# Value loads of a decode attention kernel issued from ScalarE's queue instead of SyncE's

## The chip, the core and the metric

The kernel runs on one core of a Trainium2 chip. The core has a matrix engine (TensorE, PE in the profile), VectorE (DVE), ScalarE (ACT), GpSimd (POOL) and SyncE (SP), each with its own instruction stream, and 16 DMA engines that move data from the device's memory (HBM) to the on-chip memory SBUF. SyncE and ScalarE can both issue DMAs; the profile calls SyncE's DMA queue q1 and ScalarE's q10. An engine's instructions run in order, so an engine that waits for a semaphore holds up everything behind the wait. The metric is the device time of one execution in microseconds (us). Three runs of the kernel before gave 1324.48, 1324.66 and 1324.93 us.

## The reference

Two attention branches, A and B, work on the same one-token input and are mixed by a gate:

```python
def branch(x, k_cache, v_cache, wq, wo):             # x (2, 1, 512), caches (2, 32, 4096, 128)
    q = (x @ wq).reshape(B, 1, 32, 128).transpose(0, 2, 1, 3)
    scores = einsum("bhqd,bhkd->bhqk", q, k_cache) * 128 ** -0.5
    o = einsum("bhqk,bhkd->bhqd", softmax(scores), v_cache)
    return o.transpose(0, 2, 1, 3).reshape(B, 1, 4096) @ wo

g = sigmoid((x * gate_w).sum(-1, keepdims=True))
out = g * branch(x, A_...) + (1 - g) * branch(x, B_...)
```

There is one query per head, and no key or value is used twice: 2 branches x 2 batch rows x 32 heads x 4096 tokens x 128 floats, for keys and for values, are read once each. With the four weight matrices of 8.39 MB that makes 570.43 MB.

## The kernel before

**Units.** The work is cut into 32 units, numbered 0 to 31: branch A first, then B; within a branch eight groups of four heads, and for each group the two batch rows. So an even unit is batch row 0 of a group, the odd unit after it batch row 1 of the same group. A unit has one load of keys, K(u), and one of values, V(u). Each is 4 heads x 4096 tokens x 128 floats, 8.39 MB, laid out as 128 partitions with one contiguous row of 64 KB in each.

**Tiles.** Keys have two tiles, `kt0` and `kt1`, used in turn by even and odd units. Values have one, `vt`. The same three tiles hold weights at the ends: `wq` of A and B lies in the key tiles before the first keys, `wo` of A and B in `kt0` and `kt1` after the last keys.

**What a unit does.** VectorE multiplies the key tile by the spread-out query in place (L391) and adds along the head dimension (L394); as soon as that is done it raises `k_free` for the tile. It then finds the maximum (L399 to L401) and raises `maxima`. ScalarE, on `maxima`, computes the four exponentials (L365) into `padded` and raises `weights`. TensorE, in the loop `products`, waits for `weights` and for `v_landed`, multiplies `padded` and the value tile in 32 chunks into the PSUM tile `vp` (L369; the profile shows two matmuls for each chunk), and raises `summed`. ScalarE, on `summed`, clears the used part of `padded` (L431), and tells that `vt` is free.

**Pairs.** After an odd unit ScalarE also takes the first quarter of the result out of `vp` (L452, `take_out`) and raises `taken`. VectorE, after scoring the *next* even unit, waits for `taken`, adds the other three quarters (L415, `add_out`), raises `added`, and only then looks for the maximum of the even unit and starts the next scoring. ScalarE clears `vp` on `added` (L459). So VectorE can be at most one unit ahead of the products at that point. In the middle of an even unit, between its two long instructions, VectorE waits for `spare`, which ScalarE raises after the products of the even unit before.

**The order of loads.** All large loads are issued by SyncE, in one list written out by hand: `wq` A, `wq` B, K0, K1, V0, then K2, V1, K3, V2 and so on to K31, V30, then `wo` A, V31 in three pieces (1/2, 3/8 and 1/8 of it), `wo` B in six pieces. Ahead of each K(u) SyncE waits for the `k_free` of unit u - 2, ahead of each V(u) for `v_free`, which says that V(u - 1) was used up. While SyncE waits for one tile, the loads behind it in the list aren't issued. ScalarE issues two small loads at the start (`A_x` and `gate_w`) and half of the output at the end.

**The end.** When the last products are done, VectorE, TensorE and ScalarE gather the heads, deal them out into rows and multiply by `wo` of B, whose pieces arrive last; the results are copied out and stored.

Of the kernel before, what the change touches and what calls it, by code (L numbers as in the profile page):

```python
# [12 lines left out]
P = 128  # L13
B = 2
# [4 lines left out]
G = 4  # L19
PH = P // G  # L20
NG = H // G
NS = SK // PH
NH = NS // 4
# [22 lines left out]
class Streams:  # L46
# [32 lines left out]
    def put(self, e, make, reads=(), writes=(), gives=None):  # L79

        self.before(e, reads, writes)
        i = make(self.engines[e])
        if gives is not None:
            i.then_inc(gives, 1)
            return None
        self.ticks[e] += 1
        i.then_inc(self.sems[e], 1)
        point = self.sems[e], self.ticks[e]
        self.after(point, reads, writes)
        return point  # L90
# [51 lines left out]
def tile_gated_decode(ctx: ExitStack, tc: tile.TileContext, ins: dict, out: bass.AP):  # L142
    nc = tc.nc
# [5 lines left out]
    NU = len(units)  # L149
# [5 lines left out]
    slot = small.tile([P, VC], F32, name="slot")  # L155
# [14 lines left out]
    vt = big.tile([P, NS, DH], F32, name="vt")  # L170
# [8 lines left out]
    with tc.tile_critical():  # L179
        S = Streams(nc, tc)  # L180
# [3 lines left out]
        r_vt = R()  # L184
# [6 lines left out]

        sem = tc.alloc_semaphore
        v_landed, k_landed = sem("v_landed"), [sem(f"k_landed{i}") for i in range(2)]
        v_free, k_free = sem("v_free"), [sem(f"k_free{i}") for i in range(2)]
        weights, summed = sem("weights"), sem("summed")
        maxima, taken, added, spare = sem("maxima"), sem("taken"), sem("added"), sem("spare")
        D_, A_ = Round(S, "dve"), Round(S, "act")


        def tokens(cache, u):  # L200
            n, g, b = units[u]
            rows = ins[n + cache].rearrange("b h s d -> (b h s) d")
            r0 = (b * H + g * G) * SK
            return rows[r0:r0 + G * SK].rearrange("(p r) d -> p r d", p=P)
# [2 lines left out]
            [("wq", "A"), ("wq", "B"), *(("k", u) for u in range(NU)), ("wo", "A"), ("wo", "B")])}  # L207
        parts = {}

        def load_parts(item, t, src, slots, *cuts):  # L210
            parts[item] = [S.dma("sp", t[:, i:j], src[:, i:j], slot=s) for s, i, j in zip(slots, cuts, cuts[1:])]

        def arrived(e, item, *which):
            p = parts[item]
            S.wait(e, [p[k] for k in which] if which else p)
# [6 lines left out]
        def load_k(u):  # L222
            if u == 0:
                S.before("sp", [], r_kt[0])
                load_parts(("k", 0), kt[0], tokens("_k_cache", 0), "de", 0, NS // 2, NS)
                return
            if u == 1:
                S.before("sp", [], r_kt[1])
            else:
                nc.sync.wait_ge(k_free[u % 2], u // 2)  # L230
            nc.sync.dma_start(kt[u % 2], tokens("_k_cache", u)).then_inc(k_landed[u % 2], 16)

        def load_v(u):
            if u == 0:
                S.before("sp", [], [r_vt])
            else:
                nc.sync.wait_ge(v_free, u)
            if u < NU - 1:
                nc.sync.dma_start(vt, tokens("_v_cache", u)).then_inc(v_landed, 16)
            else:  # L240
                load_parts(("v", u), vt, tokens("_v_cache", u), "deg", 0, NS // 2, NS - NH // 2, NS)

        def load_wo(n):
            i = place["wo", n]
            nc.sync.wait_ge(k_free[i], NU // 2)
            t = kt[i].rearrange("p r d -> p (r d)").rearrange("p (r e) -> p r e", e=D)
            for r in r_kt[i]:
                r.writers, r.readers = [], []
            load_parts(("wo", n), t, ins[n + "_wo"].rearrange("(p r) e -> p r e", p=P), *(
                ("f", 0, OR) if n == "A" else ("abchij", 0, OR // 2, 3 * OR // 4, EARLY, OR - 2, OR - 1, OR)))  # L250


        class Scratch:
# [3 lines left out]
            def take(self, n):  # L257
                self.at += -(-n // 128) * 128
                return self.t[:, self.at - -(-n // 128) * 128:][:, :n]

        start = Scratch(vt).take
        rows, ident, ones, xg, w, e = start(D), start(P), start(1), start(B * KC), start(P), start(1)
# [3 lines left out]
        def vput(e, make, reads=(), writes=(), **kw):  # L266
# [6 lines left out]
                                  slot="y"))  # L273
# [87 lines left out]
        def exps(u, b, col, do):  # L361

            s, m = sc[u % 2], nm[u % 2]
            for j, h in enumerate(QUARTERS):
                do(lambda x: x.activation(padded[h, :, b, j * VC:(j + 1) * VC], s[h].rearrange("p (c a) -> p c a", a=VC),  # L365
                                          AF.Exp, bias=m[h], accum_out=lp[h, col]), weights if j == G - 1 else None)
# [40 lines left out]
        def dve_second(nxt):  # L407
            take("dve", k_landed[1], 16)
            maxima_of(1, whole_scores(1, 0))
            return next_queries(*nxt, 0) if nxt else 0  # L410
# [19 lines left out]
        def clear_padded(b):  # L430
            return A_.do(lambda x: x.activation(padded[:, :, b], nil[:, :, None].to_broadcast([P, NVC, G * VC]), AF.Copy))  # L431

        def act_exps(u, b, col):
            take("act", maxima)
            exps(u, b, col, lambda make, gives: A_.do(make, 0, gives))

        def act_second(col, last=False):
            take("act", summed)
            at = clear_padded(0)
            A_.tell(v_free, at)  # L440
            A_.tell(spare, at)
            if not last:
                act_exps(1, 1, col)
                return
            A_.close()
            take("act", maxima)
            exps(1, 1, col, lambda make, gives: put("act", make, [], [R()]))
            r_lp.writers = r_pad.writers = [(S.sems["act"], S.ticks["act"])]

        def take_out(g):  # L450
            take("act", summed)
            A_.do(lambda x: x.activation(vs[:, g], vp[:, :DH], AF.Copy, scale=slot[:, :1]), 0, taken)  # L452

        def act_first(g, col, between=None):
            take_out(g)
            at = clear_padded(1)
            A_.tell(v_free, at)
            take("act", added)
            A_.do(lambda x: x.activation(vp, nil.to_broadcast([P, VC * DH]), AF.Copy))  # L459
            if between:  # L460
                between()
            act_exps(0, 0, col)
            A_.close()
# [12 lines left out]
        def deal_out(n):  # L476
            t = vs[:, 0]
            put("act", lambda x: x.activation(t, heads, AF.Copy, scale=rs), [r_heads, r_rs], [r_vs[0]])
            dealt = bank[:, :B * OR].rearrange("p (b r) -> p b r", b=B)
            for b in range(B):  # L480
                for k in range(DQ):
                    put("pe", lambda x: x.matmul(dealt[:, b], deal[:, b, k].rearrange("p g h q -> p (g h q)"),
                                                 t[:, k * OR:(k + 1) * OR], start=k == 0, stop=k == DQ - 1),
                        [r_deal, r_vs[0]], [r_bank])
            put("act", lambda x: x.activation(on[n], dealt.rearrange("p b r -> p r b"), AF.Copy), [r_bank], [r_on[n]])
# [31 lines left out]
        load_k(0)  # L517
        project("B")
        load_k(1)
        load_v(0)  # L520
        for u in range(2, NU):
            load_k(u)
            load_v(u - 1)
        load_wo("A")
        load_v(NU - 1)
        load_wo("B")

        spread_queries(0)
        for h in (0, 1):
            t = kt[0][:, h * NS // 2:(h + 1) * NS // 2]  # L530
            r = R()
# [16 lines left out]
        def dve_pairs(n):  # L548
            S.wait("dve", [*r_q.writers, (S.sems["dve"], S.ticks["dve"])])
            with nc.Fori(0, NG - 1, engines=[mybir.EngineType.DVE]) as i:  # L550
                nxt = n, bass.ds(i + 1, 1)
                at = dve_second(nxt)
                dve_first(i, nxt, at)

        def act_pairs():
            with nc.Fori(0, NG - 1, engines=[mybir.EngineType.Activation]) as i:
                act_second(bass.ds(i * B + 1, 1))
                act_first(i, bass.ds(i * B + B, 1))

        products(NU // 2)  # L560
        dve_pairs("A")
        act_pairs()
        at = dve_second(("B", slice(0, 1)))
        act_second(slice(PH // 2 - 1, PH // 2))

        def branch_sums():
            sum_of("A")
# [2 lines left out]
                gather(g)  # L570

        dve_first(NG - 1, ("B", slice(0, 1)), at, branch_sums)
        act_first(NG - 1, slice(0, 1), lambda: deal_out("A"))
        products(NU // 2 - 1)
        project_out("A", OR)
        dve_pairs("B")
        act_pairs()
        dve_second(None)
        act_second(slice(PH // 2 - 1, PH // 2), last=True)
        D_.close()  # L580

        end = Scratch(kt[place["wo", "A"]]).take
# [33 lines left out]
        for i, e in enumerate(("dve", "act")):  # L616
            for j in range(STRIPS // OS):
                k = (i * STRIPS // OS + j) * QT
                src = acc[i][k:k + B, :D // STRIPS]
# [27 lines left out]
```

## Time and profile before

| | |
|---|---|
| median of 3 runs | 1324.66 us (1324.48 to 1324.93) |
| profiled execution, its own time | 1324.58 us |
| its span, first to last instruction | 1322.8 us |
| VectorE busy | 1166.3 us (88%) |
| TensorE busy with matmuls | 343.3 us (26%) |
| ScalarE busy | 101.4 us (8%) |
| read from HBM | 570.43 MB, 431 GB/s over the span |
| q1 (SyncE's loads) | 99.6% of the time of the 16 DMA engines |
| mean granted TensorE clock | 0.627 |

Times in timelines are microseconds from the start of the span, first the start and then the duration. In rows of instructions the names stand as output<-input; an x and a number is a count; the bracket at the end gives the idle time of the engine ahead of the instruction and what ended it. SPq and ACTq are the moments at which SyncE and ScalarE issue a DMA, not the transfer. In the list of DMA issues the last number is the median time from issue to landing. DVEq, ACTq and PEq as releasers stand for an engine's own instruction stream, in which a wait for a semaphore sits. L95 and L132 are helpers that wait and signal, so rows that name them tell which engine was waited for, not for which step.

### The profile page before, as it was taken

The page shows a single profiled execution, that of the slowest core. Times are in us where ns is not written, and L with a number is a line of the kernel's source. Part 1 is how long each engine was busy: PE and PEld are TensorE (multiplying, and loading weights), DVE is VectorE, ACT ScalarE, POOL GpSimd, SP SyncE. Part 2 cuts the span into 40 slices and gives each one's busy share as a digit, 9 for nine tenths or more (in the row PEclk, how much of TensorE's full clock was granted, in tenths as well). Part 3 has the DMA queues.
Part 4 walks back from the last instruction along what each step waited for, and adds up shares of the span by engine and source line. Part 5 has one row for each costly group of instructions (what it writes and reads, how often), then busy time and mean ns, then how long its engine had stood idle before and what let it go on. Part 6 is the DMA issues. An engine that isn't in the chain of part 4 may idle for free. (4 is left out here: it accounts for less than half of the span.)

```text
span 1322.8 us, 6257 instructions
## 1 busy us (share of the span) xinstructions
PE 343.3 (26%) x2406; PEld 100.7 (8%) x2406; DVE 1166.3 (88%) x321; ACT 101.4 (8%) x331; POOL 1.2 (0%) x8
## 2 busy tenths in 40 slices
PE   3202222202222221222224022222212222221256
PEld 0000000000000000000002000000000000000012
DVE  2399999999999999999999899999999999999960
ACT  0000000001010000101000010100001010000100
POOL 0000000000000000000000000000000000000000
PEclk9656666556666655666665566666566666656668
DMA  9999999999999999999999999999999999999998
GB/s 412 442 414 442 442 416 442 444 414 444 442 430 428 442 442 416 442 442 416 444 442 419 438 442 434 426 440 440 420 440 440 420 442 442 426 432 442 434 420 357
DMA packets 11109, 570.53 MB, mean 431 GB/s; under 512 B 1239, under 2 KB 1243, under 8 KB 1630
## 3 DMA queue, kind: packets, MB, share of 16 engines
q1 hardware_dynamic: 11092, 570.43, 99.6%
q8 instruction: 4, 0.07, 0.0%
q14 instruction: 3, 0.02, 0.0%
q10 hardware_dynamic: 10, 0.01, 0.0%
HBM read 570.43 MB, written 0.00 MB: 431 GB/s over the span
## 5 line engine op out<-in xcount | busy, mean ns | idle before, releaser
L391 DVE TENSOR_TENSOR kt<-kt,q 128x16384 f32<-128x16384 f32 x31 | 534.0, 17226 | 56.1 <-DVEq L95 56.0
L394 DVE TENSOR_REDUCE sc<-kt 128x128 f32<-128x16384 f32 x31 | 533.8, 17220 | 1.1
L369 PE MATMUL vp<-vt,pr 128*32 128x512 f32 x2048 | 291.8, 733 | 919.3 <-PEq L95 918.5
L369 PEld LDWEIGHTS vp<-vt,pr 128*32 128x32 f32 x2048 | 80.3, 132 | 1129.3 <-issue 1126.9
L365 ACT ACTIVATE pr<-sc,nm 32x128 f32<-32x128 f32 x128 | 50.9, 398 | 160.0 <-ACTq L95 118.2
L431 ACT ACTIVATE pr<-nil 128x512 f32<-128x512 f32 x31 | 19.3, 624 | 426.4 <-ACTq L95 426.4
L452 ACT ACTIVATE vs<-vp,slot 128x128 f32 (+1 forms) x16 | 5.9, 368 | 451.6 <-ACTq L95 451.6
L339 PE MATMUL qa<-kt,cols 128*2 128x512 f32 x128 | 18.7, 741 | 22.9 <-DMA kt<-in_B_wq_dram 15.7
L365 ACT ACTIVATION_READ_ACCUMULATOR pr<-sc,nm (+1 forms) x128 | 23.5, 184 | 0.0
L350 DVE STREAM_TRANSPOSE kt<-kt 128x1024 f32<-128x1024 f32 x1 | 1.2, 1246 | 23.5 <-ACT kt L348 23.5
L415 DVE SCALAR_TENSOR_TENSOR vs<-vp,slot,vs 128x128 f32 (+1 forms) x45 | 15.8, 351 | 6.3 <-DVEq L95 5.3
L534 DVE TENSOR_REDUCE sc<-kt 128x64 f32<-128x8192 f32 x2 | 17.4, 8686 | 0.1
L533 DVE TENSOR_TENSOR kt<-kt,q 128x8192 f32<-128x8192 f32 x2 | 17.4, 8686 | 0.0
L459 ACT ACTIVATE vp<-nil 128x512 f32<-128x512 f32 x15 | 9.0, 600 | 106.6 <-ACTq L95 106.6
L621 DVE COPY kt<-qa 2x128 f32<-2x128 f32 x2 | 0.6, 280 | 17.0 <-PE qa L512 17.0
L592 DVE TENSOR_REDUCE kt<-kt 128x32 f32<-128x128 f32 x1 | 0.4, 368 | 12.8 <-POOL kt L590 12.8
L497 PE MATMUL most<-kt,onA 128*2 128x512 f32 x64 | 8.6, 698 | 9.5 <-DMA kt<-in_A_wo_dram 9.5
L399 DVE TENSOR_REDUCE rm<-sc 128x1 f32<-128x128 f32 x31 | 8.7, 282 | 2.3
L405 DVE STREAM_TRANSPOSE q<-qsel 128x128 f32<-128x128 f32 x30 | 9.3, 311 | 1.3 <-DVE qsel L404 0.3
L602 DVE SCALAR_TENSOR_TENSOR vs<-vp,slot,vs 128x128 f32<-128x128 f32 x3 | 1.1, 352 | 10.6 <-DVEq L95 10.6
L350 DVE STREAM_TRANSPOSE vt<-vt 128x1024 f32<-128x1024 f32 x1 | 1.2, 1246 | 9.4 <-ACT vt L348 9.4
L497 PE MATMUL most<-kt,kt 128*2 128x512 f32 x56 | 8.6, 779 | 2.4 <-DMA kt<-in_B_wo_dram 2.4
(68 smaller groups left out, 72.9 us busy)
## 6 DMA issues: line engine op xcount, KB each, us to landing
kt<-in_A_wq_dram SPq DMA_DIRECT2D x2, 4096.0 KB, 16.6
kt<-in_A_k_cache_dram SPq DMA_DIRECT2D x2, 4096.0 KB, 29.0
vt<-in_B_v_cache_dram SPq DMA_DIRECT2D x1, 4096.0 KB, 18.3
kt<-in_B_wo_dram SPq DMA_DIRECT2D x1, 4096.0 KB, 33.1
vt<-in_B_v_cache_dram SPq DMA_DIRECT2D x1, 3072.0 KB, 25.2
kt<-in_B_wo_dram SPq DMA_DIRECT2D x1, 2048.0 KB, 37.5
vt<-in_B_v_cache_dram SPq DMA_DIRECT2D x1, 1024.0 KB, 27.2
kt<-in_B_wo_dram SPq DMA_DIRECT2D x1, 1024.0 KB, 39.5
```

Source lines behind the costliest of these rows:

```text
L339: put("pe", lambda x: x.matmul(t[h * QT:h * QT + B], cols[:, c], halves[:, c, i, h], start=c == 0, stop=c == KC - 1), [r_cols, *r_kt[i_k]] ...
L365: do(lambda x: x.activation(padded[h, :, b, j * VC:(j + 1) * VC], s[h].rearrange("p (c a) -> p c a", a=VC), AF.Exp, bias=m[h], accum_out=l ...
L369: return x.matmul(vp[c % STRIPS * QT:(c % STRIPS + 1) * QT], padded[:, c].rearrange("p b m -> p (b m)"), vt[:, c * VC:(c + 1) * VC].rearra ...
L391: at = D_.do(lambda x: x.tensor_tensor(kt[o], kt[o], q[:, None, :].to_broadcast([P, NS, DH]), op=ALU.mult), after)
L394: at = D_.do(lambda x: x.tensor_reduce(sc[o], kt[o], axis=AX.X, op=ALU.add), at)
L405: return D_.do(lambda x: x.transpose(q, qsel[:, 0].to_broadcast([P, DH // QT, QT])), at)
L415: at = D_.do(lambda x: x.scalar_tensor_tensor(vs[:, g], vp[:, a * DH:(a + 1) * DH], slot[:, a:a + 1], vs[:, g], op0=ALU.mult, op1=ALU.add) ...
L431: return A_.do(lambda x: x.activation(padded[:, :, b], nil[:, :, None].to_broadcast([P, NVC, G * VC]), AF.Copy))
L459: A_.do(lambda x: x.activation(vp, nil.to_broadcast([P, VC * DH]), AF.Copy))
L497: put("pe", lambda x: x.matmul(most[s * QT:s * QT + B], on[n][:, r], wo[n][:, r], start=n == "A" and r < STRIPS, stop=n == "B" and r >= EA ...
L533: put("dve", lambda x: x.tensor_tensor(t, t, q[:, None, :].to_broadcast([P, NS // 2, DH]), op=ALU.mult), [r_q], [r])
L534: put("dve", lambda x: x.tensor_reduce(sc[0][:, h * NS // 2:(h + 1) * NS // 2], t, axis=AX.X, op=ALU.add), [r], [R()])
```

## The change

The value loads V1 to V31 leave SyncE's list. ScalarE issues V(u + 1) itself right after it has cleared `padded` for unit u: in `act_second` after even units, in `act_first` after odd ones. The semaphore `v_free` is gone, and with it SyncE's waits on it. Inside the loops over pairs the address of the load is computed from the loop's counter. V0 stays with SyncE. V31 keeps its three pieces, which ScalarE issues one after the other. SyncE's list is now `wq` A, `wq` B, K0, K1, V0, K2 to K31, `wo` A, and then a new wait: it issues the pieces of `wo` B after the second piece of V31 has landed. The bytes, the tiles and the computation are the same.

```diff
-        def load_v(u):
-            if u == 0:
-                S.before("sp", [], [r_vt])
-            else:
-                nc.sync.wait_ge(v_free, u)
-            if u < NU - 1:
-                nc.sync.dma_start(vt, tokens("_v_cache", u)).then_inc(v_landed, 16)
-            else:
-                load_parts(("v", u), vt, tokens("_v_cache", u), "deg", 0, NS // 2, NS - NH // 2, NS)
+        def load_v0():
+            S.before("sp", [], [r_vt])
+            nc.sync.dma_start(vt, tokens("_v_cache", 0)).then_inc(v_landed, 16)
+
+        def load_v(n, b, g):
+
+            rows = ins[n + "_v_cache"].rearrange("b (g h) s d -> b g (h s) d", h=G)[b, g]
+            nc.scalar.dma_start(vt, rows.rearrange("o (p r) d -> p (o r) d", p=P)).then_inc(v_landed, 16)
+
+        def load_last_v():
+            load_parts(("v", NU - 1), vt, tokens("_v_cache", NU - 1), "deg", 0, NS // 2, NS - NH // 2, NS, e="act")
...
-        def act_second(col, last=False):
+        def act_second(col, v, last=False):
             take("act", summed)
             at = clear_padded(0)
-            A_.tell(v_free, at)
             A_.tell(spare, at)
+            if last:
+                load_last_v()
+            else:
+                load_v(*v)
...
-        def act_first(g, col, between=None):
+        def act_first(g, col, v, between=None):
             take_out(g)
-            at = clear_padded(1)
-            A_.tell(v_free, at)
+            A_.wait(clear_padded(1))
+            load_v(*v)
             take("act", added)
...
-        load_v(0)
+        load_v0()
         for u in range(2, NU):
             load_k(u)
-            load_v(u - 1)
         load_wo("A")
-        load_v(NU - 1)
-        load_wo("B")
...
-        def act_pairs():
+        def act_pairs(n):
             with nc.Fori(0, NG - 1, engines=[mybir.EngineType.Activation]) as i:
-                act_second(bass.ds(i * B + 1, 1))
-                act_first(i, bass.ds(i * B + B, 1))
+                act_second(bass.ds(i * B + 1, 1), (n, 1, bass.ds(i, 1)))
+                act_first(i, bass.ds(i * B + B, 1), (n, 0, bass.ds(i + 1, 1)))
...
-        act_second(slice(PH // 2 - 1, PH // 2), last=True)
+        act_second(slice(PH // 2 - 1, PH // 2), None, last=True)
+        arrived("sp", ("v", NU - 1), 1)
+        load_wo("B")
```

More of the change, by code (lines that the diff above doesn't have):

```diff
@@ L193, in tile_gated_decode @@
         v_landed, k_landed = sem("v_landed"), [sem(f"k_landed{i}") for i in range(2)]
-        v_free, k_free = sem("v_free"), [sem(f"k_free{i}") for i in range(2)]
+        k_free = [sem(f"k_free{i}") for i in range(2)]
         weights, summed = sem("weights"), sem("summed")
@@ L208, in tile_gated_decode, with load_parts @@
         parts = {}
-        def load_parts(item, t, src, slots, *cuts):
-            parts[item] = [S.dma("sp", t[:, i:j], src[:, i:j], slot=s) for s, i, j in zip(slots, cuts, cuts[1:])]
+        def load_parts(item, t, src, slots, *cuts, e="sp"):
+            parts[item] = [S.dma(e, t[:, i:j], src[:, i:j], slot=s) for s, i, j in zip(slots, cuts, cuts[1:])]
         def arrived(e, item, *which):
@@ L553, in dve_pairs @@
                 dve_first(i, nxt, at)
-        def act_pairs():
+        def act_pairs(n):
             with nc.Fori(0, NG - 1, engines=[mybir.EngineType.Activation]) as i:
-                act_second(bass.ds(i * B + 1, 1))
-                act_first(i, bass.ds(i * B + B, 1))
+                act_second(bass.ds(i * B + 1, 1), (n, 1, bass.ds(i, 1)))
+                act_first(i, bass.ds(i * B + B, 1), (n, 0, bass.ds(i + 1, 1)))
         products(NU // 2)
         dve_pairs("A")
-        act_pairs()
+        act_pairs("A")
         at = dve_second(("B", slice(0, 1)))
-        act_second(slice(PH // 2 - 1, PH // 2))
+        act_second(slice(PH // 2 - 1, PH // 2), ("A", 1, slice(NG - 1, NG)))
         def branch_sums():
@@ L572, in tile_gated_decode @@
         dve_first(NG - 1, ("B", slice(0, 1)), at, branch_sums)
-        act_first(NG - 1, slice(0, 1), lambda: deal_out("A"))
+        act_first(NG - 1, slice(0, 1), ("B", 0, slice(0, 1)), lambda: deal_out("A"))
         products(NU // 2 - 1)
@@ L576, in tile_gated_decode @@
         dve_pairs("B")
-        act_pairs()
+        act_pairs("B")
         dve_second(None)
-        act_second(slice(PH // 2 - 1, PH // 2), last=True)
+        act_second(slice(PH // 2 - 1, PH // 2), None, last=True)
+        arrived("sp", ("v", NU - 1), 1)
+        load_wo("B")
         D_.close()
```

## The prediction

> **What bounds the kernel now.** I read the page first (span, slices, queues), then the window away from both ends, then the waits of SyncE's queue, then the timeline of one pair of units.
>
> ```profile
> span 1322.8 us, 6257 instructions
> ...
> q1 hardware_dynamic: 11092, 570.43, 99.6%
> ...
> q10 hardware_dynamic: 10, 0.01, 0.0%
> ```
> ```profile
> 120.00:1200.00 1080.00, 264.43 (x1824) 77.76 (x1824) 1016.23 (x248) 84.98 (x283) 0.00 (x0) 0.61 1.00 434
> ```
> ```profile
> SPq L239 <- ACTq L132: 958.3, 30, 34.6
> SPq L231 <- DVEq L132: 163.5, 29, 14.1
> ```
>
> The 16 DMA engines are the bound. The second fence (busy columns, clock, DMA share, GB/s) shows a share of 1.00 at 434 GB/s for 1080 us. 570.43 MB at 434 GB/s are 1314 us of the 1322.8 us span, so at most 9 us could ever be won without faster transfers. Practically everything goes through q1, SyncE's queue; q10, ScalarE's, carries 0.01 MB. SyncE spends 958.3 us waiting to be told that the value tile is free and 163.5 us for key tiles.
>
> One load (128 x 16384 float32, 8.39 MB) takes 8.39 / 0.434 = 19.3 us. A unit needs one of keys (K) and one of values (V), a pair of units four: 77.3 us. The other engines in one pair, K4 to K6:
>
> ```profile
> 199.95 0.33 SPq L231 DMA_DIRECT2D kt<-in_A_k_cache_dram  x1
> ...
> 201.26 17.23 DVE L391 TENSOR_TENSOR kt<-kt,q 128x16384 f32<-128x16384 f32 x1
> 217.44 9.26 PE L369 MATMUL vp<-vt,pr 128*32 128x512 f32 x64 [28.82 <-PEq L95]
> 218.52 17.22 DVE L394 TENSOR_REDUCE sc<-kt 128x128 f32<-128x16384 f32 x1
> 226.93 0.37 ACT L452 ACTIVATE vs<-vp,slot 128x128 f32 x1 [23.91 <-ACTq L95]
> 227.19 0.62 ACT L431 ACTIVATE pr<-nil 128x512 f32<-128x512 f32 x1
> 227.88 0.33 SPq L239 DMA_DIRECT2D vt<-in_A_v_cache_dram  x1
> 235.83 0.33 SPq L231 DMA_DIRECT2D kt<-in_A_k_cache_dram  x1
> 236.10 1.12 DVE L415 SCALAR_TENSOR_TENSOR vs<-vp,slot,vs 128x128 f32 x3 [0.35 <-DVEq L95]
> ...
> 239.01 17.23 DVE L391 TENSOR_TENSOR kt<-kt,q 128x16384 f32<-128x16384 f32 x1 [0.69 <-DVEq L95]
> 256.12 8.69 PE L369 MATMUL vp<-vt,pr 128*32 128x512 f32 x64 [29.43 <-PEq L95]
> ...
> 265.67 0.33 SPq L239 DMA_DIRECT2D vt<-in_A_v_cache_dram  x1
> 273.58 0.33 SPq L231 DMA_DIRECT2D kt<-in_A_k_cache_dram  x1
> ...
> 275.43 17.23 DVE L391 TENSOR_TENSOR kt<-kt,q 128x16384 f32<-128x16384 f32 x1 [0.57 <-DVEq L95]
> ```
>
> What to see: values land at 217.44 and 256.12 (TensorE starts then), 38.7 us apart, two loads exactly. The next value load is issued 10.44 us after an odd unit's landing (217.44 to 227.88) and 9.55 us after an even one's (256.12 to 265.67). These are holes in the value stream, but there is no hole in the DMA: a key load always stands in the same queue in front of the value load. VectorE needs 275.43 - 201.26 = 74.2 us for the pair, 3 us less than the DMA's 77.3, and waits. After an even unit's scores it also waits for `taken`, the evacuation of the odd unit before: TensorE's landing at 217.44 gives it at 227.3, VectorE comes at 236.1, so a value load has only 8.8 us to spare there.
>
> **The change, part by part.**
>
> *Issues moved to ScalarE.* 30 value loads and the three pieces of the last leave SyncE's queue for ScalarE's. A small load at the start shows what an issue costs ScalarE:
>
> ```profile
> 0.96 0.87 SPq L104 DMA_DIRECT2D kt<-in_A_wq_dram  x2
> ...
> 1.52 0.23 ACTq L104 DMA_DIRECT2D vt<-in_gate_w_dram  x1
> ...
> 8.21 0.61 PE L283 MATMUL bank<-vt 3*128 3x3 f32 x4 [8.21 <-DMA vt<-in_gate_w_dram]
> ...
> 22.71 3.62 PE L339 MATMUL qa<-kt,cols 128*2 128x512 f32 x32 [0.24 <-DMA kt<-in_A_wq_dram]
> ```
> ```profile
> kt<-in_A_wq_dram SPq DMA_DIRECT2D x2, 4096.0 KB, 16.6
> ```
>
> 30 + 3 issues at 0.23 (this one) to 0.33 us (SyncE's for the same load) are 8 to 11 us of ScalarE. Behind each stand the next exponentials, which wait for VectorE's maxima anyway (it idled 23.91 us ahead of the evacuation above): 0 on the path; without that cover, up to 11. No row shows the register arithmetic of an address that moves with the loop; from below 0, from above one more issue each (0.33 us), off the path likewise; I take 0. The message to SyncE that goes away saves about 0.1 us per load (227.19 + 0.62 to 227.88), at most 3 in all, and lies in the issue latency below.
>
> *Who goes first in the DMA engines.* This decides the case. Before, order of landing is order of issue. Now K and V are in flight from two queues at once. The trace has one such meeting. `gate_w` (2 KB, ScalarE's queue) was issued at 1.52, after the first 4 MB half of `wq` (SyncE's, 0.96), and TensorE had it at 8.21. The second half of `wq` was there at 22.71, which is 21.3 us after its issue at about 1.4; with a median of 16.6 over the two, the first took 11.9 and landed at 12.9. So the later load passed the earlier one: the queues share the engines, they do not stand in one line. It still took 6.7 us for 2 KB, so it got no precedence either. I take equal turns, half the rate each while both hold full loads (rows of 64 KB on both sides). The Trainium skill, "DMA: Bandwidth & Descriptors", Queues, rings and completion order, states that each DMA engine goes round-robin between the queues it has work for, a packet at a time; the order of landing above agrees, and the 6.7 us are longer than a single turn.
>
> *What sharing does to a pair.* A load alone has 22.71 - 0.96 - 19.3 = 2.4 us of start and completion around two halves. Let an odd V land at W.
> - Its products and evacuation: the next (even) V is issued at W + 10.44. Meanwhile K for the next even unit is in flight (VectorE freed its tile before W, below), so the DMA stays full. K and V together hold 38.6 us of work: the even V lands at W + 38.6, the K well before (12 us alone, the other 7.3 at half rate: W + 27).
> - `taken` comes at W + 9.9; from there 236.10 to 239.01, 2.9 us, to the next scoring, which takes 34.5: VectorE frees the next key tile at W + 47.3. The odd V is issued 9.55 us after the even landed, at W + 48.2. Between W + 38.6 and those issues *both* queues are empty. The hole is 8.7 to 9.55 us and the 2.4 us of starting: **11.1 to 12.0 us of idle DMA per pair**, about 11.5.
> - K and V, issued together, then share from the start and land together after 2.4 + 38.6 us: the odd V is at W + 89, VectorE has scored another unit by W + 47.3 + 1.9 + 34.5 = W + 84 and waits for `taken`. That frees its tile 5 us ahead of the landing, which is the K in flight of the first step. The pair closes at 88.4 to 89.3 us against 77.3.
>
> *How often.* Before, a V took from 227.88 to 256.12, 28.2 us; beside a full K it takes up to 41, so V falls behind by up to 13 us a load, and the 8.8 us spare are gone within a few units. V2 to V30 give at most 15 such holes; the first two or three pairs are on the way there, with holes of 0 to 4 us while V slips. I count 12 full holes and half a one in all: 12.5 x 11.5 = 144.
>
> *The end.*
>
> ```profile
> 1232.08 0.33 SPq L239 DMA_DIRECT2D vt<-in_B_v_cache_dram  x1
> ...
> 1271.57 1.28 SPq L104 DMA_DIRECT2D vt<-in_B_v_cache_dram  x3
> 1276.21 4.70 SPq L104 DMA_DIRECT2D kt<-in_B_wo_dram  x6
> ...
> 1309.31 8.57 PE L497 MATMUL most<-kt,kt 128*2 128x512 f32 x56 [2.38 <-DMA kt<-in_B_wo_dram]
> ```
>
> `wo` of B was issued at 1276.21, long before its turn. Now SyncE waits until 7/8 of the last V have landed; the last 1 MB is 2.4 us of DMA against 2.4 of starting: 0 to 2.4 lost, I take 1. Behind that wait stand only the `wo` pieces and the output. `wo` of A takes the place of a K beside V30, so the last hole counts as the others, and the tail from 1309.31 on is unchanged.
>
> *Sum.* 144 + 1 = 145 us on the profiled execution, whose time is 1324.58 (1.8 us outside the span), 0.1 from the median of 1324.66: **1470 us**, 11% slower. Bounds of this case: 10 holes of 11.1 with nothing at the end, 1436; 15 of 12.0 and 2.4, 1507. As the transition does cost something, I put its own range at 1440 to 1495.
>
> **Rivals.**
> - *Nothing changes.* If the queues in effect serve by order of issue, V and K land as before; the price is the end's 0 to 2.4 us: 1325. For it: order of issue hardly changes, since SyncE was already waiting for the same events; the small load's 6.7 us look like some queueing. Against: the 2 KB load passed 4 MB. The Trainium skill, same page, section "Issuing engines are not separate DMA queues", says that issuing from several engines saves only the sequencer's time; read as a forecast, that is this rival, while the first rule speaks for mine.
> - *Values favoured.* With a share s of the engines, V's round trip is 10 us of products and issue, 2.4 of starting and 19.3/s; it fits into the 38.65 us of a unit from s = 0.74. From three turns in four on, V lands within 29 us of its issue, `taken` comes in time, and K fills the holes. The DMA stays full; what remains is keys up to one load later at the end, since the last scoring frees the tile for `wo` of B: 0 to 19 us, about 1335. Nothing shows such a favour.
> - *Keys favoured.* SyncE's queue, deeper most of the time, gets more turns; V then waits out the K and the hole comes after nearly every pair from the start: 15 x 12 = 180, 1500.
> - *Faster.* If two queues let an engine overlap the turn from one row to the next, the rate would rise above 434 GB/s while both are in flight, 28.2 of 38.7 us (73%). With no holes, x% of rate gives 0.73x%: it shows from x = 0.3%, and stops at VectorE's 74.2 us per pair, 15.5 x 3.1 = 48 us, 1277. Against it: 16 engines at a share of 1.00 for 1080 us show no gap between loads to be filled, and any equal sharing brings the holes with it.
>
> **How the numbers follow.** About 0.2% (2.6 us) is what a measurement here can tell from none. Equal turns 0.74 (1440 to 1495); between equal and values favoured, or V favoured outright, 0.08 (1330 to 1440, slower); keys favoured 0.06 (about 1500); order of issue 0.08, nearly all within 0.2%; faster 0.03; 0.01 for others, slower. Faster 0.03, same 0.08, slower 0.89. The range takes in the first case with the keys' rival and the upper part of the middle one, 1405 to 1502, and leaves out somewhat under 0.2.
>
> **What would show it.** q10 carries 31 value loads, about 260 MB. The DMA share falls to 0.87 to 0.90 over the middle, with one hole of about 11 us per pair, each right after an even unit's values land. V landings alternate 38 to 39 and 49 to 51 us apart. VectorE's `taken` wait before L415 grows from 0.35 to about 13 us per pair; its scoring keeps 17.2 us an instruction. K loads take up to 41 us with V in flight. Wrong would be: no dip in the slices (order of issue, or V favoured: whether a V lands ahead of a K issued before it tells which), holes from the first pairs on with V at 45 us and more (K favoured), or a rate well above 434 GB/s while both run.

## The result and the profile after

The changed kernel takes 1496.32 us (median of 4 runs, 1490.65 to 1499.0) against 1324.68 us: a ratio of 1.129, 95% interval 1.1256 to 1.1324. That is 13% slower; the prediction was 1470 us. The profiled execution is the fastest of the four: it took 1490.65 us, its span is 1488.9.

The DMA share in 40 slices before (first fence), and from the page of the changed kernel its span, the same share, and the queues (packets, MB, share of the 16 engines):

```profile
DMA  9999999999999999999999999999999999999998
```
```profile
span 1488.9 us, 6285 instructions
...
DMA  9999899699896979969797996979979796997968
...
q1 hardware_dynamic: 6340, 310.38, 48.6%
q10 hardware_dynamic: 4762, 260.06, 40.7%
```

The slices, all 9 but the last before, now drop to 6 and 7 at regular distances. The two queues together use 89.3% of the engines, 1329.6 us of 1488.9. Before it was 99.6% of 1322.8, 1317.5 us. So the 166.1 us of longer span are 154 us in which DMA engines had nothing to do, and 12.1 us in which the same bytes took longer.

The pair of units of the changed kernel that the prediction's pair answers to, timeline (start, duration, bracket: idle before):

```profile
598.66 9.51 PE L371 MATMUL vp<-vt,pr 128*32 128x512 f32 x64 [40.98 <-PEq L95]
...
609.01 1.12 DVE L417 SCALAR_TENSOR_TENSOR vs<-vp,slot,vs 128x128 f32 x3 [18.21 <-DVEq L95]
609.45 0.34 ACTq L240 DMA_DIRECT2D vt<-in_A_v_cache_dram  x1
...
629.16 17.22 DVE L396 TENSOR_REDUCE sc<-kt 128x128 f32<-128x16384 f32 x1
634.89 8.46 PE L371 MATMUL vp<-vt,pr 128*32 128x512 f32 x64 [26.73 <-PEq L95]
...
644.38 0.34 ACTq L240 DMA_DIRECT2D vt<-in_A_v_cache_dram  x1
...
683.16 9.92 PE L371 MATMUL vp<-vt,pr 128*32 128x512 f32 x64 [39.80 <-PEq L95]
...
693.92 1.12 DVE L417 SCALAR_TENSOR_TENSOR vs<-vp,slot,vs 128x128 f32 x3 [11.67 <-DVEq L95]
...
713.83 17.22 DVE L396 TENSOR_REDUCE sc<-kt 128x128 f32<-128x16384 f32 x1
724.28 9.84 PE L371 MATMUL vp<-vt,pr 128*32 128x512 f32 x64 [31.20 <-PEq L95]
...
735.01 0.35 ACTq L240 DMA_DIRECT2D vt<-in_A_v_cache_dram  x1
```

Odd values land at 598.66 and 683.16, even ones at 634.89 and 724.28: the distances are 36, 48 and 41 us, where each was 38.7. VectorE sits 18.21 and 11.67 us in front of L417, waiting for `taken`; the key tile that it would free next stays taken. After the even landing at 634.89 the next loads are the value load at 644.38 and the key load when VectorE has scored, at 629.16 + 17.22 = 646.38. After the one at 724.28 the key load is first (713.83 + 17.22 = 731.05) and the value load follows at 735.01. Stretches of the same kernel, busy columns as before (PE, PEld, DVE, ACT, POOL), then clock, DMA share and GB/s; a DMA packet counts where it starts, and the stretches of the first fence begin when the last packet before them has ended:

```profile
634.50:645.33 10.83, 8.46 (x64) 2.42 (x64) 10.83 (x1) 0.63 (x1) 0.00 (x0) 0.85 0.00 0
723.90:732.07 8.17, 7.79 (x48) 2.27 (x52) 7.92 (x6) 0.00 (x0) 0.00 (x0) 0.63 0.00 0
...
sum 140.73, PE 121.85 PEld 34.78 DVE 138.05 ACT 5.28 POOL 0.00; mean PE 8.12 PEld 2.32 DVE 9.20 ACT 0.35 POOL 0.00
```
```profile
600.00:634.00 34.00, 8.17 (x60) 2.13 (x52) 24.11 (x10) 3.45 (x11) 0.00 (x0) 0.60 1.00 432
```

Here is the lost time: 10.8 and 8.2 us without a byte moved, around the landings of even units, and 432 GB/s, hardly less than before, between them. The sum is over all fifteen such holes of the kernel, one to a pair: the first has 3.75 us, the others 6.83 to 12.39, together 140.73. The whole of VectorE's wait, from the lists of waits before and after:

```profile
DVE vs L415 <- DVEq L95: 5.3, 15, 0.4
```
```profile
DVE vs L417 <- DVEq L95: 217.4, 15, 21.8
```

### The profile page after: what moved, and what is told of

It is laid out like the page before. It is cut to its first block, busy times and chain, and to the rows that moved or that the text cites. A ratio compares the mean times of both kernels' runs of the same rounds, so it can differ in the third digit from the quotient of the medians.

```text
span 1488.9 us, 6285 instructions
## 1 busy us (share of the span) xinstructions
PE 341.3 (23%) x2406; PEld 98.0 (7%) x2406; DVE 1166.2 (78%) x321; ACT 101.3 (7%) x331; POOL 1.2 (0%) x8
## 5 line engine op out<-in xcount | busy, mean ns | idle before, releaser
L371 PE MATMUL vp<-vt,pr 128*32 128x512 f32 x2048 | 296.0, 742 | 1099.3 <-PEq L95 1096.0
L417 DVE SCALAR_TENSOR_TENSOR vs<-vp,slot,vs 128x128 f32 (+1 forms) x45 | 15.8, 351 | 218.5 <-DVEq L95 217.4
L433 ACT ACTIVATE pr<-nil 128x512 f32<-128x512 f32 x31 | 19.3, 624 | 530.7 <-ACTq L95 530.7
L464 ACT ACTIVATE vp<-nil 128x512 f32<-128x512 f32 x15 | 9.0, 600 | 14.5 <-ACTq L95 14.5
L402 DVE STREAM_TRANSPOSE across<-rm 128x32 f32<-128x32 f32 x31 | 6.6, 212 | 1.1
## 6 DMA issues: line engine op xcount, KB each, us to landing
vt<-in_B_v_cache_dram ACTq DMA_DIRECT2D x1, 4096.0 KB, 13.2
vt<-in_B_v_cache_dram ACTq DMA_DIRECT2D x1, 1024.0 KB, 22.3
```

Source lines behind the costliest of these rows:

```text
L371: return x.matmul(vp[c % STRIPS * QT:(c % STRIPS + 1) * QT], padded[:, c].rearrange("p b m -> p (b m)"), vt[:, c * VC:(c + 1) * VC].rearra ...
L417: at = D_.do(lambda x: x.scalar_tensor_tensor(vs[:, g], vp[:, a * DH:(a + 1) * DH], slot[:, a:a + 1], vs[:, g], op0=ALU.mult, op1=ALU.add) ...
```

## The experiments

The theory: two queues take turns in the DMA engines, row by row. A value load therefore takes up to twice as long beside a key load, VectorE has to wait for it, and once per pair both queues run empty. Rivals: the engines share by bytes and not by rows; ScalarE as issuer, or the wait at the end, is what costs; two queues lower the transfer rate.

**Row size as the dose.** Keys cut into four, two or three DMAs, so that their rows are 16, 32 or 21 KB beside the values' 64 KB; `k_quarters`:

```diff
-            nc.sync.dma_start(kt[u % 2], tokens("_k_cache", u)).then_inc(k_landed[u % 2], 16)
+            src = tokens("_k_cache", u)
+            for j in range(0, NS, NH):
+                nc.sync.dma_start(kt[u % 2][:, j:j + NH], src[:, j:j + NH]).then_inc(k_landed[u % 2], 16)
...
-            take("dve", k_landed[1], 16)
+            take("dve", k_landed[1], 64)
```

`k_halves` steps by NS // 2 and `k_thirds` cuts at 43 and 86 of 128; VectorE waits for 32 and 48.

> The changed kernel, with each key load from K1 on cut into four DMAs of 16 KB per partition; value loads keep rows of 64 KB on ScalarE's queue. Theory (turns by row: where both queues hold loads, a DMA engine takes a row from each in turn): values now get 64 of every 80 KB, a share of 0.8, above the 0.74 from which their round trip fits into a unit. The holes go: 1325 to 1345 us, DMA share 0.99 or more in the middle. Rival (shares by bytes or time, however the rows are cut): nothing changes, 1480 to 1505 with a share of 0.89. Rival (the price lies in ScalarE as issuer, or in the last weights' wait): 1480 to 1505 as well.

Measured: 1339.73 us, 1.0104 times before (1.008 to 1.0128). Its queues, its wait for `taken`, and 1000 us of its middle:

```profile
q1 hardware_dynamic: 19732, 310.39, 54.5%
q10 hardware_dynamic: 4762, 260.06, 44.8%
...
L419 DVE SCALAR_TENSOR_TENSOR vs<-vp,slot,vs 128x128 f32 (+1 forms) x45 | 15.8, 351 | 6.3 <-DVEq L95 5.3
```
```profile
300.00:1300.00 1000.00, 246.32 (x1708) 72.09 (x1704) 925.86 (x220) 76.89 (x254) 0.00 (x0) 0.62 1.00 430
```

The turns can be counted, too. These are the packets that started while both queues held full loads, first in the changed kernel (652 to 676 us), then with quarters (624 to 643 us):

```profile
q1 hardware_dynamic: 80, 5.24, 50.4%
q10 hardware_dynamic: 80, 5.24, 50.4%
```
```profile
q10 hardware_dynamic: 96, 6.29, 76.4%
q1 hardware_dynamic: 97, 1.46, 17.9%
```

As many packets from the one queue as from the other, whatever their size: that is the turn by row, seen directly. The bytes go half and half in the first fence, 81 to 19 in the second.

Same two queues, same issuer, same bytes in each, and 157 of the 172 us are back: no hole in the middle, and the wait for `taken` is at the 5.3 us that it was before the change. This excludes sharing by bytes, ScalarE as issuer and the wait at the end as the main cause; a lower rate of two queues is no more than the 12.1 us above.

> The changed kernel with each key load from K1 on cut into two DMAs of 32 KB per partition; value rows stay at 64 KB. Theory (turns by row): values have 2/3 of the engines beside a key load, less than the 0.74 from which they keep up, more than 1/2. An odd V then lands 31 us after its issue instead of 41, VectorE waits for it some 5 us instead of 13, and the hole of a pair shrinks from 11.5 to 2 to 5 us: 1355 to 1395 us. Rival (a share is enough or it is not, by some other threshold): 1325 to 1345, or 1480 to 1505.

Measured: 1433.16 us (1.0831, 1.0794 to 1.0868), between the two, but 38 us above the top of the expected range. Two rows of its timeline tell part of why, the issue and the landing of an odd unit's values; behind them the packets that started from 613.99 to 618.30:

```profile
613.99 0.34 ACTq L242 DMA_DIRECT2D vt<-in_A_v_cache_dram  x1
...
647.06 9.82 PE L373 MATMUL vp<-vt,pr 128*32 128x512 f32 x64 [34.09 <-PEq L95]
```
```profile
q1 hardware_dynamic: 48, 1.57, 84.5%
```

33.1 us instead of the sum's 31.4 (2.4 + 19.3 / (2/3)). The load joins keys that are already in flight, and loses some 2 us in doing so: in the 4.3 us behind its issue only key rows start, three for each engine, where the values that were issued into a hole at 644.38 in the changed kernel started 1.0 us later, at the hole's end.

> The changed kernel with each key load from K1 on in three DMAs of 21 to 21.5 KB rows: values have a share of 0.75 beside a key load. By the prediction's sum (10 + 2.4 + 19.3/s has to fit into 38.65 us) that is just enough: no holes, 1330 to 1350 us. With halves of the keys, though, an odd V took 33 us from issue to landing and not 31, as if it lost 2 us more in joining; with 2 us more the round trip is 40.1 us, 1.5 too long, VectorE has to wait a little in each pair and small holes stay: 1350 to 1400.

Measured: 1369.69 us (1.0343, 1.0313 to 1.0373). The second figure was right: with 2 us for joining, three quarters aren't enough. VectorE's wait for `taken` follows the dose:

```profile
DVE vs L419 <- DVEq L95: 72.3, 15, 9.2
```
```profile
DVE vs L419 <- DVEq L95: 146.3, 15, 15.0
```

72.3 us with thirds (first fence), 146.3 with halves (second), 5.3 with quarters, 217.4 uncut. The times go the same way: 1340, 1370, 1433, 1496.

**The opposite dose.** `v_quarters` cuts the values in the same manner (V0 too) and leaves the keys whole.

```diff
-            nc.scalar.dma_start(vt, rows.rearrange("o (p r) d -> p (o r) d", p=P)).then_inc(v_landed, 16)
+            src = rows.rearrange("o (p r) d -> p (o r) d", p=P)
+            for j in range(0, NS, NH):
+                nc.scalar.dma_start(vt[:, j:j + NH], src[:, j:j + NH]).then_inc(v_landed, 16)
...
-                take("pe", v_landed, 16)
+                take("pe", v_landed, 64)
```

> The changed kernel, with each value load cut into four DMAs of 16 KB per partition; keys keep rows of 64 KB. Theory (turns by row): values get a share of 0.2 beside a key load. After an odd landing the even V is last to land in any case and the pair keeps its one hole; after an even landing it waits out the keys as well. Fewer shared pairs in the run-up, so a little more: 1495 to 1545. Rival (shares by bytes): as the changed kernel, 1485 to 1505, with four issues of 0.3 us more on ScalarE hidden. Rival (four smaller loads cost transfer rate by themselves): slower in proportion to bytes, with a DMA share that stays where it was, 0.89, and fewer GB/s.

Measured: 1523.97 us (1.1506, 1.1487 to 1.1525), inside the theory's range: worse, but not by much. The theory's reason, that an uncut pair already has its one hole, fits: from 286 us on each pair has one long stretch without a byte here, too, of 7.6 to 12.3 us.

**What small rows cost alone.** The kernel before, one queue, with the diff of `k_quarters`.

> The kernel before, all loads in SyncE's queue and in the old order, with each key load from K1 on cut into four DMAs of 16 KB rows. It tells what the smaller rows cost by themselves, of the 15 us that the changed kernel with such rows stood above the kernel before. From the 16 KB rows of the weights in the profiles (0.611 us each, against a quarter of a 64 KB row's 2.419, 0.605) the keys' half of the bytes takes 1% longer: 1328 to 1333 us. Rival (rows cost nothing, all 15 us are the end, where the last keys land later): 1324 to 1326.

Measured: 1328.4 us (1.0028, 1.0018 to 1.0039), 3.8 us above before. So of the 15 us of `k_quarters` about 4 are rows. For the rest, the two profiled executions differ by 13.5 us of span: by the queues' shares 5.4 us are longer transfers (last section) and 8.1 us idle engines, most of that at the end. The last landings and issues of `k_quarters`:

```profile
1272.38 8.88 PE L373 MATMUL vp<-vt,pr 128*32 128x512 f32 x64 [31.59 <-PEq L95]
...
1282.14 1.31 ACTq L104 DMA_DIRECT2D vt<-in_B_v_cache_dram  x3
1289.29 17.22 DVE L398 TENSOR_REDUCE sc<-kt 128x128 f32<-128x16384 f32 x1
...
1308.90 3.56 SPq L104 DMA_DIRECT2D kt<-in_B_wo_dram  x6
```

The values of unit 30 land at 1272.38, and those of unit 31 are issued at 1282.14, 10.6 us later than before (1271.57). The last key tile is free at 1306.5; `wo` of B is issued 2.4 us behind that, at 1308.90 (1276.21 before), so it waited for the second piece of V31 and not for the keys.

**Who issues.** The kernel before with value loads on GpSimd's queue (TensorE's loop over units is written out and counts landings, the pieces of V31 have semaphores of their own, and `wo` of B waits as in the changed kernel):

```diff
-                nc.sync.wait_ge(v_free, u)
+                nc.gpsimd.wait_ge(v_free, u)
             if u < NU - 1:
-                nc.sync.dma_start(vt, tokens("_v_cache", u)).then_inc(v_landed, 16)
+                nc.gpsimd.dma_start(vt, tokens("_v_cache", u)).then_inc(v_landed, 16)
```

> The kernel before with the value loads issued by GpSimd, which waits for the old message that the tile is free and does nothing else; ScalarE keeps its old work, and the last weights wait for the last values as in the changed kernel. Theory (a second queue beside SyncE's is the cause, whoever issues): the pairs get their holes, 1470 to 1510 if this queue's turns are rows too; if its rows are cut smaller, values get fewer turns and it is 1495 to 1545. Rival (ScalarE as issuer is the cause): 1324 to 1330.

Measured: 1513.06 us (1.1425, 1.1406 to 1.1444).

```profile
q0 software_dynamic: 4896, 268.44, 41.3%
```

ScalarE issues nothing large here, and the loss is there all the same. A second queue is the cause, not its owner. GpSimd's queue is of another kind, but its rows are whole: 31 x 128 of V0 to V30, 3 x 128 of the pieces of V31 and 34 x 16 tiny packets make the 4896. For whole rows the range ended at 1510, 3 us too low; what GpSimd as issuer adds was not separated.

**The end alone, and the change without its end.** `tail_only` adds the wait to the kernel before; `no_tail_wait` takes the same line out of the changed kernel.

```diff
         load_v(NU - 1)
+        arrived("sp", ("v", NU - 1), 1)
         load_wo("B")
```

> The kernel before, all loads in SyncE's queue in their old order, with only the new wait: the pieces of B's output weights are issued once 7/8 of the last values have landed. Theory: 0 to 2.4 us more than before, 1324.7 to 1327.1. Rival (the wait at the end is a good part of the loss): 1330 or more.

Measured: 1325.69 us, 1.0008 (0.9998 to 1.0017): 1 us, not clear of none.

> The changed kernel without the wait ahead of B's output weights: they are issued as soon as the last key tile is free and share the engines with the last values. Theory: the holes stay, and the last values land later for the sharing, with some 20 us of work behind them: 0 to 15 us more than the changed kernel, 1490 to 1515. Rival (the wait is a good part of the loss): 1470 or less.

Measured: 1507.89 us (1.1388, 1.1369 to 1.1407), 12 us slower than the changed kernel. The last piece of V31 takes 38.3 us from issue to landing (second fence) where it took 22.3 in the changed kernel (first fence):

```profile
vt<-in_B_v_cache_dram ACTq DMA_DIRECT2D x1, 1024.0 KB, 22.3
```
```profile
vt<-in_B_v_cache_dram ACTq DMA_DIRECT2D x1, 1024.0 KB, 38.3
```

The wait is worth having, because it keeps the last weights from sharing with the last values.

**Shortening and lengthening the hole.** `half_early` lets TensorE signal after half of its products, and ScalarE then issues the first half of the next values:

```diff
-            nc.scalar.dma_start(vt, rows.rearrange("o (p r) d -> p (o r) d", p=P)).then_inc(v_landed, 16)
+            part = slice(h * NS // 2, (h + 1) * NS // 2)
+            nc.scalar.dma_start(vt[:, part], rows.rearrange("o (p r) d -> p (o r) d", p=P)[:, part]).then_inc(v_landed, 16)
...
+            take("act", halfway)
+            load_v(*v, 0)
             take_out(g)
```

> The changed kernel with each value load from V1 to V30 in two DMAs of 32 KB rows, the first issued by ScalarE when TensorE is halfway through the products before, the second where the whole load stood. Theory (the loss is the hole after an even landing, in which both queues are empty): the hole ends 4.5 to 5 us earlier, so 15 x 4.7 = 70 us of the changed kernel's 172 come back: 1410 to 1445. What goes against it: the smaller rows give values a third of the turns beside a key load, which the odd V pays for; then 1440 to 1490. Rival (ScalarE as issuer is the price): 16 pairs of issues more cost time instead, 1496 or more.

Measured: 1485.25 us (1.1206, 1.1188 to 1.1225), 11 us gained. Two stretches of one pair, behind the even and behind the odd landing:

```profile
637.37:644.08 6.71, 6.27 (x48) 1.96 (x52) 6.71 (x1) 0.00 (x0) 0.00 (x0) 0.75 0.00 0
684.01:687.22 3.21, 2.79 (x16) 0.92 (x20) 2.19 (x1) 0.00 (x0) 0.00 (x0) 0.50 0.00 0
```

The hole is shorter, 6.7 us, and a second one of 3.2 us stands at the odd landing. What the early issue gave was mostly given back. The time is in the range of the expectation's second case, but not shown to be for its reason, the values' smaller share: by the queues' shares (49.0% and 40.9% of 1485.3 us) the engines idle 150 us against 159 in the changed kernel, so the second holes take back most of what the first ones gave, and the transfers take 5.7 us more.

`even_late` repeats ScalarE's clear ten times more, each behind the one before it; `odd_late` does the same to `clear_padded(1)`:

```diff
-            at = clear_padded(0)
+            at = clear_padded(0, 11)
```

> The changed kernel with ten needless clears of padded more on ScalarE (0.62 us and a wait each, 7 us in all) after every even unit, ahead of the message spare and the issue of the odd unit's values. Theory: the hole after an even landing ends with the key load, which VectorE's scoring sets and not ScalarE, and the odd V is the last to land by the sum of the work, whenever it joins; so 0 to 25 us more than the changed kernel, 1490 to 1525. Rival (what ScalarE does between landing and issue is what costs): 7 us in each of 16 pairs, 110 us more, 1590 to 1615.

Measured: 1536.97 us (1.16, 1.158 to 1.1619), 41 us above the changed kernel: above the theory's range and far below the rival's.

```profile
643.50 17.22 DVE L396 TENSOR_REDUCE sc<-kt 128x128 f32<-128x16384 f32 x1
650.36 9.03 PE L371 MATMUL vp<-vt,pr 128*32 128x512 f32 x64 [27.86 <-PEq L95]
...
667.02 0.34 ACTq L240 DMA_DIRECT2D vt<-in_A_v_cache_dram  x1
...
704.51 5.83 PE L371 MATMUL vp<-vt,pr 128*32 128x512 f32 x32 [45.12 <-PEq L95]
```

The key load, free at 643.50 + 17.22 = 660.72, did end the hole as I had said, 10.4 us behind the landing at 650.36. But in the changed kernel the values were sometimes first (644.38 against 646.38), so that was given up. The odd values landed 43.8 us behind 660.72, where the sum of the work gives 2.4 + 38.6 = 41.0. The packets that started from 699.30 to 703.40 (first fence) and from 703.40 to 704.20 (second) show where the last 2.8 us are:

```profile
q1 hardware_dynamic: 16, 1.05, 59.1%
```
```profile
q1 hardware_dynamic: 16, 1.05, 302.3%
q10 hardware_dynamic: 16, 0.00, 1.1%
```

No row of values starts any more; the next key load is in flight already, and only behind one key row of each engine come sixteen tiny packets of the value queue, one for each engine. I take them for the report that the load is through: it waits for its turn like a row, and a row of 64 KB is about 2.4 us (65536 bytes at a sixteenth of 434 GB/s). The changed kernel has this wait too, ahead of the landing at 683.16, so it is no part of the 41 us. Those are idle engines: 13.2% of 1535.2 us by the queues' shares (47.5% and 39.3%), 43 us more than the 10.7% of 1488.9.

> The same ten clears more, but after every odd unit, ahead of the issue of the even unit's values and behind the message taken. Theory: a key load is in flight over that time and the DMA stays full; 0 to 25 us more than the changed kernel, 1490 to 1525. Rival (issue time on ScalarE costs): 110 us more, 1590 to 1615.

Measured: 1534.2 us (1.1571, 1.1552 to 1.1591), 38 us more, a miss too:

```profile
616.23 10.00 PE L371 MATMUL vp<-vt,pr 128*32 128x512 f32 x64 [43.47 <-PEq L95]
...
634.11 0.34 ACTq L240 DMA_DIRECT2D vt<-in_A_v_cache_dram  x1
```
```profile
632.72:635.06 2.34, 0.00 (x0) 0.00 (x0) 2.34 (x1) 1.67 (x3) 0.00 (x0) 0.50 0.00 0
```

The values are now issued 17.9 us behind the odd landing, and the keys alone in flight have run out 1.4 us before that: a second hole of 2.3 us in the pair. I had taken the cover to reach further. Both delays cost far less than the 110 us that a time spent on the path in every pair would.

## Why the prediction was right, and where its size was off

- *Nothing but the DMA bounds the kernel, no gain to be had*: right. No variant came below 1324 us.
- *Equal turns, from one 2 KB load that passed 4 MB*: right, but half the rate each was an assumption that turned out to hold; that one small load showed only that the queues share. The counted packets show the halves (80 and 80, 5.24 MB each). Turns go by row: with rows of 64 KB on one side and 16 KB on the other the holes vanish. This also agrees with the Trainium skill, "DMA: Bandwidth & Descriptors", Queues, rings and completion order, which has turns by packet; here a contiguous row of a load behaved as one.
- *The pair*: right in its course and, on average, in its length. From 598.66 to the last odd landing but one, nine pairs on, it closes at 88.4 us (forecast 88.4 to 89.3):

```profile
1394.30 9.34 PE L371 MATMUL vp<-vt,pr 128*32 128x512 f32 x64 [40.91 <-PEq L95]
```

  (1394.30 - 598.66) / 9 = 88.4. The wait for `taken` is 217.4 / 15 = 14.5 us a pair (13), the DMA share 0.89 (0.87 to 0.90). That the length fits so well is in part luck, for two sizes were off and made up for each other: the holes are 9.4 us on average (140.73 / 15) against 11.1 to 12.0, and transfers that the sum left at their old rate take longer. The single pair varies, too. The sum had keys and values issued together after the hole; in the trace now the values come first (644.38 against 646.38), now the keys (731.05 against 735.01). So the even values land mostly 36 or 41 us behind the odd ones, not 38 to 39 each time, and the odd ones 48 us and more behind the even ones (49 to 51).
- *How often, and what was left out*: together they make the difference of 1470 to 1496. I let two or three pairs pass before the full loss and counted 12.5. The trace shows fifteen holes, and only the first is small: VectorE's second wait for `taken` is already the longest,

```profile
257.36 1.13 DVE L417 SCALAR_TENSOR_TENSOR vs<-vp,slot,vs 128x128 f32 x3 [21.84 <-DVEq L95]
```

  The 8.8 us that values had to spare lasted one pair, since one shared load is up to 13 us late. More holes, each shorter: the idle engines cost 154 us (the end, and engines that run dry a little before or start a little after the others, among them) where the sum had 144 + 1. So this term was about 9 us too small. The other 12.1 us of the profiled execution's 166 are the longer transfers, which the sum had at nothing. The median lies another 5.7 us above that execution; no trace shows where.
- *ScalarE's issues at nothing*: right, by `k_quarters` and `pool_values`. *The end, 1 us*: in line with `tail_only`, whose 1 us is not clear of none.
- *The rivals*: order of issue would have left 1325. Values favoured, from a share of 0.74 on, about 1335: the mechanism is the one that `k_quarters` shows, at 1339.7, but the threshold was a little low. A share of 0.75 still lost 45 us, 30 more than a share of 0.8, because joining a busy engine costs some 2 us that the sum had left out. Keys favoured, 1500: `v_quarters`, which favours them, took 1524.

## What to carry to other kernels

When the DMA engines are the bound, the order of the loads is part of the design: a single queue holds each load back until the ones that are needed earlier are through. Before moving a stream into a second queue, work out its round trip at the share that it will get; if that no longer fits into the period, the waits for its tile leave both queues empty at the same time, as they did here. If two queues must be used: in these runs the size of the contiguous rows set the shares.

## What was not expected of the hardware

- A load's share beside another load went with its row size: with values' rows fixed at 64 KB, key rows of 64, 32, 21 and 16 KB gave 1496, 1433, 1370 and 1340 us.
- The same bytes needed 12.1 us more of the engines' time in the changed kernel (1329.6 against 1317.5 us; one step of the last digit of a share is 1.3 to 1.5 us). In `k_quarters` it is 99.3% of 1340.1 us, 1330.7, against 99.9% of 1326.6, 1325.3, for the same rows in one queue:

```profile
span 1326.6 us, 6350 instructions
...
q1 hardware_dynamic: 24484, 570.44, 99.9%
```

  So two queues cost some transfer time even without holes, here about 5 us. The reason stays open.
- A value load that joined keys in flight started 4.3 us behind its issue (`k_halves`), one that found the engines empty 1.0 us behind it (the changed kernel), and the landing of one that ended beside keys was seen 2.8 us late (`even_late`).
